# The second product of the last superblock by seven products of halves, transposed, and w_out's sums made from the second superblock on

## The chip, the cores and the metric

The kernel runs on one core of one Trainium2 chip. The metric is the device time of one execution in microseconds (us). PE is TensorE, ACT ScalarE, DVE VectorE, POOL GpSimd, and SP the engine whose queue issues all the transfers.

## What is computed

Chunk attention, then a feed-forward network with ELU, all in float32:

```
q, k, v: (8, 8, 576, 64)       chunks of 64 tokens, 8 heads
attn = softmax(q_c k_c^T / 8) over each chunk;  x = attn v_c   -> x: (4608, 512)
h = x @ w_in                   w_in: (512, 2048)
g = where(h > 0, h, exp(min(h, 0)) - 1)
out = g @ w_out                w_out: (2048, 512)
```

## The kernel before

**Tiling.** The 4608 tokens are 9 blocks of 512 (TB). A float32 product is made of three matmuls of rounded parts, high by high, high by low and low by high (`three`, L405): each operand X is kept as a cast hi and a difference lo = X - hi. The inner size 2048 is cut into 16 pieces f of 128 (NF), the model size 512 into 4 (NK).

**Stages.** The first three blocks are plain: for each f, `hidden` (L414) makes h with 12 matmuls of 512 columns, ACT and DVE make g (`elu`, L429), and `second_next` (L644) multiplies g by w_out for four token tiles, three matmuls each. The other six blocks form three superblocks of 1024 tokens (NS). There the first product is made by seven products of halves (Strassen's way, in Winograd's form) instead of eight. A pair g (class `Pair`, L596) stands for two pieces f; each of its seven products is 6 matmuls of 512 columns. The operands on w_in's side (sums of quarters) are made once by POOL in `combine` (L469), written to DRAM as `a_dram`, and loaded product by product (`load_a`, L531, line 533); those on x's side are made by `prepare` (L560). ACT copies products from PSUM (L629), DVE adds (L633), `elu_of` (L575) makes g, and `split_g` (L587) splits it, its cast on ACT (L588) and its low part (L590) on POOL or DVE.

**The second product** of a superblock is not reduced. Its first half of tokens is multiplied between the products of the pairs; its second half's g is kept in `g_kept` and multiplied after the eight pairs, under the list KEPT. `second` (L639) puts four products per f into a queue and `Q` in the lists takes the next one; eight items are still in the queue when a superblock ends, and the next one begins with them. The low half of w_out goes round through a ring of eight slices, loaded from `lo_dram` (`load_lo`, L546, line 549).

**Order.** The order of every engine except POOL's is written out by hand, in lists of items. One pair of a superblock follows

```
    PAIR = (
        "m p1 c1 4 E Q 4 z p2 d1 Q p6 c2 h 1 Q Q 1 p5 1 q k 1 Q l p7 c3 d2 Q Q 2 p4 c4 2 Q 3 p3 d3 "
        "3 3 3 s v x V"
    )
```

`p` is a product, `c` a copy, `d` an addition, `1` to `4` steps of g, `Q` a second product. The other letters are the attention of the next superblock's tokens, one tile of 128 per pair (class `Tokens`): m, E, z the softmax (L344 to L357), h the turn of the weights (L363 to L373), s the scores (L235), v the multiplication by v (L243), x its copy (L394), q and k the turns of q and k (L334), l and V the loads (L215, L199). In step h, DVE transposes blocks of 32 into `turned` (L366), ACT copies it into `unturned` (L369), and SP swaps blocks between partitions by four transfers of 32 KB, turned<-unturned (L373). PE's step v needs them. All transfers go out through SP in program order, so one that waits holds up those behind it. Loads of q and k are eight per tile (L215), sixteen where a tile crosses from one batch to the next (576 is not a multiple of 128).

The last superblock (from 667.76 us in the profile) has no attention left beside it. Its 24 left-over matmuls, 336 of the first product and 384 of the second follow the same lists. The finished tiles are copied from PSUM and stored as rows of 2 KB (`copy_out`, L446 to L449).

## Time and profile before

| | |
|---|---|
| median of 3 runs | 841.0 us (838.89 to 841.65) |
| span of the profiled execution, first to last instruction | 840.2 us |
| own time of the profiled execution beyond its span | not listed |
| PE busy | 826.3 us, 98% |
| DVE, ACT, POOL busy | 501.6, 480.4, 179.0 us |
| moved by DMA | 164.09 MB, 195 GB/s over the span |

Busy time is the time in which an engine has an instruction under way; matmuls overlap, so a busy PE says only that it was never empty. The chain of waits follows the work that ended last back to what released it. A window gives each engine's busy time between two moments.

### The profile page before, as it was taken

To read this page: it belongs to the slowest core of one execution; us is meant where nothing else is said; L and a number is where in the kernel's file an instruction comes from. 1 tells how busy PE (TensorE), PEld (TensorE's weight loads), DVE (VectorE), ACT (ScalarE), POOL (GpSimd) and SP (SyncE) were. 2 spreads that over 40 slices of the span, in tenths; PEclk is the share of its full clock that TensorE was granted. 3 is DMA by queue.
4 is the path that set the end of the run, shared out by engine and by line. 5 is a ranking of instruction groups with operands and counts; after the bars stand their busy time and mean duration, and the time that the engine had idled before them with its cause. 6 is when DMAs were issued, how large, how long until landed. Compare 5 with 4: busy or idle time off the path is not lost.

```text
span 840.2 us, 15685 instructions
## 1 busy us (share of the span) xinstructions
PE 826.3 (98%) x5949; PEld 677.0 (81%) x5949; DVE 501.6 (60%) x719; ACT 480.4 (57%) x825; POOL 179.0 (21%) x149
## 2 busy tenths in 40 slices
PE   7899999999999999999999999999999999999998
PEld 6788888887888888888888888778888888888886
DVE  4999997666775679565666746566555333233411
ACT  5999875444554547656666436655664355555521
POOL 0000014445312221111114521111126211111120
PEclk8999999999999999999999999999999999999999
DMA  9875754865787777698888656779844365545331
GB/s 240 263 228 187 247 181 152 271 205 183 232 234 218 207 193 218 191 258 239 241 240 242 191 149 200 199 233 257 238 146 138 111 198 160 164 144 163 101 101 50
DMA packets 178794, 164.09 MB, mean 195 GB/s; under 512 B 65568, under 2 KB 161312, under 8 KB 178720
## 3 DMA queue, kind: packets, MB, share of 16 engines
q1 hardware_dynamic: 178720, 163.10, 66.0%
q8 instruction: 47, 0.77, 0.4%
q14 instruction: 27, 0.22, 0.1%
HBM read 131.07 MB, written 28.31 MB: 190 GB/s over the span
## 4 chain that ended last, share of the span: by engine, by line
PE 92%; ACT 2%; DVE 2%; DMA 2%; SPq 1%; issue 1%; DVEq 0%; ACTq 0%
PE o L408 45%; PE h L408 40%; PE ps_a L235 2%; PE ps_a L243 2%; PE h L425 1%; DMA turned<-unturned 1%; SPq L199 1%; DMA k_sb<-in_k_dram 1%; PE ps_a L257 1%; PE ps_a L302 1%; SPq L373 0%; ACT st L135 0%; ACT a L280 0%; DVE e L435 0%; ACT e L433 0%
## 5 line engine op out<-in xcount | busy, mean ns | idle before, releaser
L408 PE MATMUL o<-wo_hi,ghi 128*128 128x512 f32 x416 | 163.8, 394 | 0.1
L408 PE MATMUL o<-wo_hi,glo 128*128 128x512 f32 x416 | 162.2, 390 | 0.0
L408 PE MATMUL o<-wo_lo,ghi 128*128 128x512 f32 x416 | 162.0, 390 | 0.0
L590 POOL TENSOR_TENSOR glo<-e,ghi 128x512 fp32r<-128x512 f32 x46 | 59.5, 1293 | 318.4 <-ACT ghi L588 318.4
L408 PE MATMUL h<-xhi,wi_hi 128*128 128x512 f32 x324 | 108.1, 394 | 0.0
L408 PE MATMUL h<-xlo,wi_hi 128*128 128x512 f32 x324 | 106.7, 389 | 0.0
L408 PE MATMUL o<-wo_hi,wo_lo 128*128 128x512 f32 x320 | 99.2, 389 | 0.0
L408 PEld LDWEIGHTS o<-wo_hi,ghi 128*128 128x128 f32 x416 | 78.1, 188 | 17.4 <-ACT ghi L440 0.5
L408 PEld LDWEIGHTS o<-wo_hi,glo 128*128 128x128 f32 x416 | 78.1, 188 | 16.7 <-DVE glo L443 0.4
L408 PEld LDWEIGHTS o<-wo_lo,ghi 128*128 128x128 f32 x416 | 78.1, 188 | 15.8
L629 ACT COPY kept<-h 128x512 f32<-128x512 f32 x72 | 42.2, 586 | 62.1 <-PE h L408 62.0
L408 PE MATMUL h<-wi_lo,wi_hi 128*128 128x512 f32 x288 | 75.0, 396 | 0.0
L408 PE MATMUL h<-wo_lo,wi_hi 128*128 128x512 f32 x288 | 72.9, 389 | 0.0
L408 PEld LDWEIGHTS h<-xhi,wi_hi 128*128 128x128 f32 x324 | 60.8, 188 | 12.9
L408 PEld LDWEIGHTS h<-xlo,wi_hi 128*128 128x128 f32 x324 | 60.8, 188 | 12.2
L408 PEld LDWEIGHTS o<-wo_hi,wo_lo 128*128 128x128 f32 x320 | 60.1, 188 | 12.5
L408 PE MATMUL h<-xhi,wi_lo 128*128 128x512 f32 x180 | 70.2, 390 | 0.0
L583 DVE SCALAR_TENSOR_TENSOR g_kept<-e,g_kept 128x512 f32<-128x512 f32 x48 | 33.2, 692 | 61.4 <-ACT e L580 61.4
L633 DVE TENSOR_TENSOR g_kept<-h,kept 128x512 f32<-128x512 f32 x48 | 33.1, 690 | 51.8 <-ACT kept L629 27.2
L408 PEld LDWEIGHTS h<-wo_lo,wi_hi 128*128 128x128 f32 x288 | 54.1, 188 | 11.2
L580 ACT ACTIVATE e<-e 128x512 f32<-128x512 f32 x96 | 60.7, 632 | 3.1
L408 PE MATMUL o<-wo_lo 128*128 128x512 f32 x160 | 62.2, 389 | 0.0
(114 smaller groups left out, 1330.3 us busy)
## 6 DMA issues: line engine op xcount, KB each, us to landing
wi_hi<-a_dram SPq DMA_DIRECT2D x168, 256.0 KB, 3.9
wo_lo<-lo_dram SPq DMA_DIRECT2D x52, 512.0 KB, 4.5
kept<-in_q_dram SPq DMA_DIRECT2D x100, 128.0 KB, 3.5
kept<-in_k_dram SPq DMA_DIRECT2D x100, 128.0 KB, 3.9
v_sb<-in_v_dram SPq DMA_DIRECT2D x32, 256.0 KB, 6.2
st<-in_moe_w_in_dram SPq DMA_DIRECT2D x16, 512.0 KB, 4.0
st<-in_moe_w_out_dram SPq DMA_DIRECT2D x16, 512.0 KB, 5.2
a_dram<-kept SPq DMA_DIRECT2D x16, 512.0 KB, 4.1
```

The costliest lines, as they stand in the source:

```text
L199: nc.sync.dma_start(out=dst[p0:p0 + n], in_=src[b, :, s0:s0 + n, :].rearrange("h s d -> s h d"))
L235: nc.tensor.matmul(scores[halves[c], j, hp, :], lhsT=qT[halves[j], hp, halves[c]], rhs=kT[halves[j], hp, halves[c]], start=True, stop=True,)
L243: nc.tensor.matmul(x_ps[halves[j], c, hp, :], lhsT=v_sb[halves[c], 2 * hp + j, :], rhs=aT[halves[c], :, j * NK + hp], start=True, stop=True,)
L257: nc.tensor.transpose(out=both[:, i, hp * P:(hp + 1) * P], in_=src[:, 2 * hp:2 * hp + 2, :], identity=ident,)
L302: nc.tensor.matmul(turned_ps[half, h, :], lhsT=a[half, h, :], rhs=ident[half, half], start=True, stop=True,)
L408: nc.tensor.matmul(ps, lhsT=a, rhs=b, start=start, stop=stop, skip_group_check=onto)
L425: nc.tensor.matmul(h, lhsT=w[:, kt, :], rhs=x[:, kt, :], start=i == 0, stop=i == len(terms) - 1)
L580: nc.scalar.activation(out=e, in_=e, func=AF.Exp, scale=-1.0)
L583: nc.vector.scalar_tensor_tensor(out=to, in0=e, scalar=-1.0, in1=c, op0=ALU.add, op1=ALU.max)
L590: engine.tensor_tensor(out=lo, in0=e, in1=hi.bitcast(F32), op=ALU.subtract)
L629: nc.scalar.copy(out=c21 if i == 4 else self.kept[i - 1], in_=x_ps)
L633: nc.vector.tensor_tensor(out=to, in0=y_ps, in1=self.kept[kept], op=ALU.add)
```

## The change

In the last superblock the second product too is made by seven products of halves: the token half and the two pieces f of a pair on g's side, two pieces f and two halves of the 512 columns on w_out's side. Each of the seven is 8 steps j (one per pair of pieces f) of 6 matmuls of 512 columns. w_out is the stationary operand now and g the moving one, so the result comes out transposed; DVE turns it back in blocks of 32, and to that end the columns of w_out are put in another order when it is first split (`in_order`), in all blocks. The stores of that superblock then have runs of 64 floats, in the last part of 32.

The operands on w_out's side go to a new DRAM tensor, `w_dram`. Three of the seven are raw quarters (`write_raw`, `write_raw_low`: 28 writes, item list RAW, beside KEPT of superblock 1). Four are sums (class `Sums`): for each j, POOL makes two additions of 512 columns and four subtractions of 256, ACT casts 1024 columns, DVE subtracts 1024, SP writes twice 512 KB. Those of j = 0 to 3 are made step by step in pairs 0 to 4 of superblock 1 (SUMS_AT; the writes fall behind `d2` of pairs 1 to 4), those of j = 4 to 7 at the start of the last superblock (`add_sums`).

The whole last superblock is no longer written out as a list. A class `Plan` collects jobs, each with reads, writes, an engine (or a choice of DVE and POOL) and a cost, and lays them out by list scheduling: PE in the given order, the others by the due time worked back from PE. POOL takes a job only when DVE is held by other work and the job isn't due soon, and the plan lets POOL and DVE not work at once on operations that share their way to the memory. All of the first product comes first (56 products of 6 matmuls), then the 56 steps of the second. All operands go through a ring of four entries of 512 KB (`load_entry`), loaded when the entry before has been used; the first four are loaded beside KEPT of superblock 1, in place of the loads of A there, and the last four loads of w_out's low half are no longer made. Four buffers are made differently without a change in size (`gp`, `io`), and POOL's order is by hand too from the third block on. Superblocks 0 and 1 otherwise keep their lists.

```diff
@@ -106,6 +106,10 @@
+    def in_order(w):
+
+        return w.rearrange("p (c b d) -> p b c d", b=4, d=Q)
+
...
+    HALF = DM // 2
+    w_dram = dram.tile([7, NG // 2, P, 2, 2, HALF], F32, name="w_dram")
+    W_OPS = (5, 6, 7, 4, 1, 2, 3)
+    W_PARTS = {1: (0, 0), 2: (1, 0), 3: (1, 1)}
...
 
+    class Sums:
+        def __init__(self, j: int, place, lows):
+            self.j, self.lows = j, lows
+            self.place = place.rearrange("p (l a) -> p l a", l=2)
+            self.w = self.place[:, 0].rearrange("p (i d) -> p i d", i=2)
+            self.s = self.place[:, 1].rearrange("p (i d) -> p i d", i=4)
+        def whole(self, i: int, engine=nc.gpsimd):
+            engine.tensor_tensor(
+                out=self.w[:, i], in0=w_out_slices(2 * self.j + i)[0].bitcast(F32),
+                in1=self.lows[i].bitcast(F32), op=ALU.add)
+        def sum(self, t: int, engine=nc.gpsimd):
+            b11, b12, b21, b22 = [self.w[:, i, c * HALF:(c + 1) * HALF]
+                                  for i in range(2) for c in range(2)]
+            t1, t2, t3, t4 = [self.s[:, i] for i in range(4)]
+            out, a, b = ((t1, b12, b11), (t2, b22, t1), (t3, b22, b12), (t4, b21, t2))[t - 1]
+            engine.tensor_tensor(out=out, in0=a, in1=b, op=ALU.subtract)
+        def high(self):
+            nc.scalar.copy(out=self.place[:, 0].bitcast(F32R), in_=self.place[:, 1])
+        def low(self, engine=nc.vector):
+            engine.tensor_tensor(
+                out=self.place[:, 1].bitcast(F32R), in0=self.place[:, 1], in1=self.place[:, 0],
+                op=ALU.subtract)
+        def write(self):
+            for lo in range(2):
+                nc.sync.dma_start(
+                    out=w_dram[:4, self.j // 2, :, self.j % 2, lo, :].rearrange("i p w -> p i w"),
+                    in_=self.place[:, lo].rearrange("p (i d) -> p i d", i=4))
...
+        def lows(j: int, half: int = 0):
+            return [weights[half][3][:, (2 * j + i) % (NF // 2), :] for i in range(2)]
+        for j, row in ((0, 8), (1, 12), (2, 8), (3, 12)):
+            yield j, lambda row=row: flat(g_kept[:, row:row + 4]), lows(j)
+    def write_raw(n: int, lo: int):
+        half, i = divmod(n, 3)
+        row, col = W_PARTS[i + 1]
+        for d in range(2):
+            nc.sync.dma_start(
+                out=w_dram[4 + i, 2 * half + d, :, :, lo, :],
+                in_=weights[half][2 + lo][:, 4 * d + row:4 * d + 4:2, col * HALF:(col + 1) * HALF].bitcast(F32))
+    def write_raw_low(j: int):
+        lows = weights[0][3][:, 2 * j % (NF // 2):][:, :2].bitcast(F32)
+        of = w_dram[:, j // 2, :, j % 2, 1]
+        nc.sync.dma_start(out=of[4], in_=lows[:, 0, :HALF])
+        nc.sync.dma_start(out=of[5:7].rearrange("i p d -> p i d"),
+                          in_=lows[:, 1].rearrange("p (i d) -> p i d", i=2))
     def flat(t):
         return t.rearrange("p a b -> p (a b)")
 
...
+    RAW = {0: "L0 L1", 1: "L2 L3", 2: "W0", 4: "W1", 6: "W2", 9: "L4 L5", 10: "W3", 11: "R0 L6", 12: "W4 R1",
+           13: "L7 W5", 14: "R2", 15: "R3"}
+    SUMS_AT = {0: ("p3",), 1: ("p1", "p2", "p6", "p5", "d2", "p4", "p3"),
+               4: ("p1", "p2", "c2", "d2"), 5: (), 6: (), 7: ()}
+    SUMS_AT[2] = SUMS_AT[3] = ("p1", "p2", "c2", "d2", "p4", "p3")
...
+    def load_entry(e: int):
+        slot, (phase, e) = ring_slot(e), divmod(e % ENTRIES, 7 * PAIRS)
+        if not phase:
+            d, o = divmod(e, 7)
+            for a in range(2):
+                nc.sync.dma_start(
+                    out=slot[:, a].bitcast(F32),
+                    in_=a_dram[2 * d + a, :, :, AOPS.index(PRODUCTS[FIRST[o]][0])])
+        else:
+            o, d = divmod(e, PAIRS)
+            nc.sync.dma_start(out=slot.bitcast(F32), in_=w_dram[W_OPS.index(SECOND[o]), d])
...
-    for s in range(NS):
-        n0 = (PLAIN + 2 * s) * TB
+    preparing, pair = True, None
+    for sb in range(2):
+        n0 = (PLAIN + 2 * sb) * TB
         run = n0, o_tiles(), a_half_place
...
-        preparing, kept = s + 1 < NS, iter(range(NF))
-        run = n0 + TB, o_tiles(), b_half_place
-        for line in KEPT:
-            for item in line.split():
+                if sb and item in SUMS_AT[g]:
+                    do("w")
+        halves_kept, o_last = iter(range(NF)), o_tiles()
+        run = n0 + TB, o_last, b_half_place
+        for f, line in enumerate(KEPT):
+            for item in line.split() + (RAW.get(f, "").split() if sb else []):
                 if item == "4":
                     next(pair.parts["4"], None)
                 elif item == "G":
-                    split_kept(next(kept))
+                    split_kept(next(halves_kept))
                 else:
                     do(item)
-    queue.sort(key=lambda item: item[2])
-    while queue:
-        second_next()
...
+    def product_second(i: int, j: int, e: int, s: int, to):
+        slot = ring_slot(e)[:, j % 2].rearrange("p l (i d) -> p l i d", i=2)
+        for c in range(2):
+            three(bank(to[c]), slot[:, 0, c], slot[:, 1, c], split_place(s, 0), split_place(s, 1),
+                  i in (1, 2, 4, 5) and j == 0, j == NG - 1, onto=i not in (1, 2, 4, 5))
...
+                if e == "POOL":
+                    at = max(port["DVE"], now)
+                    if at > now:
+                        return None, at
+                    aside = max(free["DVE"], now) + sum(
+                        jobs[i]["engines"]["DVE"][0] for i in ready["DVE"]
+                        if not jobs[i]["port"] and ready_at[i] <= now + POOL_NEAR)
+                    took = {i: jobs[i]["engines"]["POOL"][1] for i in mine}
+                    mine = [i for i in mine if aside >= now + POOL_SHARE * took[i] and (
+                        "DVE" not in jobs[i]["engines"] or jobs[i]["due"] >= now + POOL_MARGIN + 2 * took[i])
+                        or jobs[i]["due"] < now + 3000 and "DVE" not in jobs[i]["engines"]]
+                    if not mine:
+                        return None, later_on
+                if e == "DVE" and port["POOL"] > now:
...
+        def send():
+            for b in range(4):
+                at = b * P + c * 2 * Q
+                nc.sync.dma_start(
+                    out=out[n0:n0 + TB, at:at + 2 * Q].rearrange("(t p) d -> p t d", p=Q),
+                    in_=place()[b * Q:(b + 1) * Q].rearrange("p (t d) -> p t d", d=2 * Q))
+
...
+        def send(engine, which):
+            def run_():
+                for b in which:
+                    at = b * P + (2 + c) * Q
+                    engine.dma_start(
+                        out=out[n0:n0 + TB, at:at + Q].rearrange("(t p) d -> p t d", p=Q)[
+                            :, (cols.start or 0) // Q:cols.stop // Q],
+                        in_=place[b * Q:(b + 1) * Q])
...
+        block_of = {1: 0, 2: 1, 4: 3, 6: 3, 5: 0, 7: 2, 3: 1}
...
+            to = (x_, y_, z_)[banks_of[i]]
+            for j in range(NG):
+                k = NG * o + j
+                t, slot, b = t1 + k, k % NSPLIT, block_of[i]
...
+                ts = max(t - NSPLIT + .9, t1 + 1.2 if slot >= 4 else 0)
+                plan.add(ts, "ACT", ACT_OP, high, [("G", j, b)], [hi, lo])
+                plan.add(ts + .01, None, EITHER, low_, [("G", j, b), hi], [lo])
+                if i == 4:
+                    place2, place3 = [lambda j=j, b=b: g_place(j, b) for b in (3, 2)]
+                    place0, place1 = [lambda j=j, b=b: g_place(j, b) for b in (0, 1)]
+                    plan.add(ts + .1, None, EITHER, minus(place2, place2, place3),
+                             [("G", j, 2)], [("G", j, 3)])
+                    plan.add(ts + .2, None, EITHER, minus(place0, place0, place2, ALU.add),
+                             [("G", j, 3)], [("G", j, 0)])
+                    plan.add(ts + .3, None, EITHER, minus(place1, place1, place2),
+                             [("G", j, 3)], [("G", j, 1)])
...
+    for j in range(NG // 2, NG):
+        add_sums(T0 + 2 + 6 * (j - NG // 2), j)
+    for s in range(2, NS):
+        superblock(s)
+        if s + 1 < NS:
+            tokens(s)
+    plan.emit()
```

## Rows read from the trace of the kernel before

**Rows 1.** The page: first line, and busy us of PE

```profile
span 840.2 us, 15685 instructions
...
PE 826.3 (98%) x5949; PEld 677.0 (81%) x5949; DVE 501.6 (60%) x719; ACT 480.4 (57%) x825; POOL 179.0 (21%) x149
```

**Rows 2.** Waits of PE, 492 to 640 us: us, times, longest

```profile
PE ps_a L243 <- DMA turned<-unturned: 1.4, 3, 0.8
```

**Rows 3.** The chain of waits, whole span: start us, us, what

```profile
624.01 43.75 PE o L408 x192
...
787.44 49.03 PE o L408 x216
```

**Rows 4.** Windows: length, busy us, PEclk, DMA share, GB/s

```profile
667.76:787.44 119.68, 119.68 (x529) 99.13 (x529) 38.20 (x58) 66.52 (x112) 18.10 (x14) 1.00 0.51 153
```

**Rows 5.** Windows of pairs 2 to 5 of superblock 1, and a busy stretch

```profile
524.30:542.00 17.70, 16.86 (x135) 13.70 (x131) 10.38 (x17) 10.54 (x18) 2.95 (x3) 1.00 0.68 190
542.00:559.40 17.40, 16.81 (x131) 13.65 (x132) 10.11 (x16) 10.02 (x17) 2.35 (x3) 1.00 0.84 244
559.40:575.60 16.20, 16.20 (x131) 13.26 (x131) 9.83 (x16) 9.40 (x16) 2.45 (x2) 1.00 0.80 231
575.60:591.90 16.30, 16.30 (x135) 13.36 (x131) 10.13 (x17) 9.93 (x17) 2.59 (x2) 1.00 0.94 256
569.00:571.00 2.00, 2.00 (x11) 1.65 (x10) 2.00 (x4) 1.21 (x2) 1.11 (x1) 1.00 1.09 366
```

**Rows 6.** The chain of waits, 530 to 560 us

```profile
535.86 1.31 SPq L373
...
537.22 3.59 DMA turned<-unturned
...
553.72 4.82 DMA turned<-unturned
```

**Rows 7.** Timeline of SP, 515 to 590 us: start, us

```profile
522.95 5.24 SPq L215 DMA_DIRECT2D kept<-in_k_dram  x8
...
535.86 3.21 SPq L373 DMA_DIRECT2D turned<-unturned  x4
```

**Rows 8.** Operations by line, whole span: count, busy us, mean ns, idle before

```profile
L473 POOL TENSOR_TENSOR kept<-kept 128x256 f32<-128x256 f32 x32 | 29.2, 932 | 1.3
...
L473 POOL TENSOR_TENSOR kept<-wi_hi,wi_lo 128x512 f32<-128x512 f32 x16 | 21.3, 1350 | 157.4 <-DMA kept<-in_k_dram 117.2 <-DMA a_dram<-kept 40.1
L366 DVE STREAM_TRANSPOSE turned<-ps_a 128x512 f32<-128x512 f32 x28 | 20.1, 716 | 1.0
...
L502 DVE TENSOR_TENSOR kept<-kept 128x1024 fp32r<-128x1024 f32 x8 | 11.5, 1443 | 1.8 <-ACT kept L501 1.6
...
L172 ACT CAST wo_hi<-xf 128x512 fp32r<-128x512 f32 x16 | 10.0, 623 | 1.4 <-DVE xf L168 1.4
...
L590 DVE TENSOR_TENSOR wo_lo<-g_kept,wo_lo 128x512 fp32r<-128x512 f32 x11 | 7.6, 690 | 27.7 <-ACT wo_lo L588 27.7
```

**Rows 9.** Line L507, the writes of combine's sums: issue ns, and landing

```profile
L507 SPq DMA_DIRECT2D a_dram<-kept x16: 332/376/506, 153.0 to 257.9; - x16
...
DMA to landing us min/median/max: 2.8/4.1/6.0
```

**Rows 10.** Timeline of the end, 826 to 841 us

```profile
836.50 0.69 DVE L448 COPY g_kept<-o 128x512 f32<-128x512 f32 x1 [1.96 <-PE o L408]
```

**Rows 11.** Line L449, the last stores, from 780 us: issue ns, and landing

```profile
L449 SPq DMA_DIRECT2D out_dram<-g_kept x4: 332/334/337, 833.0 to 837.2; - x4
...
DMA to landing us min/median/max: 2.0/2.0/3.0
```

**Rows 12.** Line L199, whole span, loads of v: issue ns, and landing

```profile
L199 SPq DMA_DIRECT2D v_sb<-in_v_dram x40: 383/570/3506, 3.8 to 593.2; - x40
...
DMA to landing us min/median/max: 3.1/5.6/7.4
```

**Rows 13.** Line L443, the low part of g: ns min, median, max

```profile
L443 DVE TENSOR_TENSOR glo<-e,ghi x35: 642/692/1842, 35.6 to 322.7; 128x512 fp32r<-128x512 f32 x35
```

More of the change, by code (lines that the diff above doesn't have):

```diff
@@ new lines, in combine_w_out, with sums_by_hand @@
+    def combine_w_out():
+        for j, place, lows in sums_by_hand():
+            sums = Sums(j, place(), lows)
+            sums.whole(0)
+            yield
+            sums.whole(1)
+            yield
+            sums.sum(1)
+            sums.sum(3)
+            yield
+            sums.sum(2)
+            sums.sum(4)
+            yield
+            sums.high()
+            yield
+            sums.low()
+            sums.write()
+            yield
+    def sums_by_hand():
+        def lows(j: int, half: int = 0):
+            return [weights[half][3][:, (2 * j + i) % (NF // 2), :] for i in range(2)]
+        for j, row in ((0, 8), (1, 12), (2, 8), (3, 12)):
+            yield j, lambda row=row: flat(g_kept[:, row:row + 4]), lows(j)
@@ L593, in g_tiles @@
     def g_tiles():
-        return [gp.tile([P, TB], F32R, name=name) for name in ("ghi", "glo")]
+        return [place_of_g(F32R, name) for name in ("ghi", "glo")]
     class Pair:
@@ L843 @@
     later_w_out = w_out_tiles(wo1)
-    gp = ctx.enter_context(tc.tile_pool(name="gp", bufs=2, reuse_waits="tile"))
+    gp = ctx.enter_context(tc.tile_pool(name="gp", bufs=1, reuse_waits="tile"))
+    for i in range(6):
+        unit(i, F32, "unused")
     plain = ctx.enter_context(ExitStack())
@@ new lines, in add_attention, with now, score_, v_of @@
+    def add_attention(t: float, n: int, last: int):
+        tile_n = later.get(n)
+        this = {}
+        def now():
+            return later[n]
+        if n <= last:
+            def score_():
+                later[n].score()
+            plan.add(t, "PE", (590, 800), score_, ["qT", "kT"], ["psa"])
+        before = later.get(n - 1)
+        def v_of():
+            later[n - 1].times_v()
+        def x_of():
+            later[n - 1].keep()
+        half, part = divmod((n - 1) % (2 * NTT) ^ NTT, NTT)
+        cols = "a" if part < NTT - 1 else "b"
+        plan.add(t + .01, "PE", (590, 800), v_of, ["turned", ("v", (n - 1) % 2)], ["psa", "xps"])
+        plan.add(t + .7, "ACT", ACT_PSUM, x_of, ["psa", "xps"],
+                 [(name, part) for name in (("b11", "b21") if half == 0 else ("b12", "b22"))])
+        if n <= last:
+            add_softmax(t, n)
@@ new lines, in add_sums, with begin @@
+    def add_sums(t: float, j: int):
+        made = {}
+        def begin(engine):
+            made[0] = Sums(j, g_more_of(4 + j % 2), [weights[0][3][:, 2 * j + i - NF // 2, :] for i in range(2)])
+            made[0].whole(0, engine)
+        place = [("G", 4 + j % 2, b) for b in range(4)]
+        raw = [("s", i, l) for i in range(4) for l in range(2)] + [
+            ("G", i, b) for i in (6, 7) for b in range(4)]
+        half = {"DVE": (350, 423), "POOL": (700, 740)}
+        plan.add(t, None, EITHER, begin, raw, place[:1])
+        plan.add(t + .1, None, EITHER, lambda engine: made[0].whole(1, engine), raw, place[1:2])
+        for i, (k, reads) in enumerate(((1, ()), (3, ()), (2, (("t", j, 1),)), (4, (("t", j, 2),)))):
+            plan.add(t + .2 + .1 * i, None, half, lambda engine, k=k: made[0].sum(k, engine),
+                     [*place[:2], *reads], [("t", j, k)] + (place[2:] if k == 1 else []))
+        plan.add(t + .7, "ACT", (955, 1047), lambda: made[0].high(),
+                 [("t", j, k) for k in range(1, 5)] + place[2:], place[:2])
+        plan.add(t + .8, None, either(2 * TB), lambda engine: made[0].low(engine), place[:2], place[2:])
+        plan.add(t + .9, "SP", dma(2, 3200), lambda: made[0].write(), place, [("sums", j)])
```

632 lines of the change are left out of this document (573 added, 59 removed).

## The prediction, made before the change was run

> **What bounds the kernel now.** I read the page first: PE is busy 826.3 of 840.2 us and has 5949 matmuls [rows 1]; with so little idle time only two things can move the time, fewer matmuls or new waits of PE. The list of PE's waits comes second: in the pairs of superblock 1 it holds one entry, for the transfers turned<-unturned, 1.4 us in three places [rows 2]. The chain of waits comes third. It shows what a matmul of 512 columns costs in a row without a gap: 43.75 us for 192 and 49.03 us for 216 [rows 3], so 0.227 us. The last superblock begins at 667.76 (624.01 + 43.75) and its last matmul ends at 836.47 (787.44 + 49.03). By the code it holds 24 left-over matmuls, 336 of the first product and 384 of the second, 744 in all; 744 x 0.227 is 168.9 us against 168.7 measured. PE is busy 119.68 of 119.68 us in its first part [rows 4]. That stage is purely a count of matmuls, and ACT (66.5 us) and DVE (38.2 us) are half idle in it.
>
> The windows by pair of superblock 1 come fourth, since the change puts work there. Pairs 2 and 3 last 17.70 and 17.40 us, with PE busy 16.86 and 16.81; pairs 4 and 5 have no idle PE, though the DMA engines are busy 0.80 and 0.94 of the time [rows 5]. The chain around pairs 2 and 3 says why: PE stood before the multiplication with v until the four small swap transfers (L373) landed, 3.59 and 4.82 us after their issue [rows 6]. SP's timeline shows the cause: a token tile that crosses a batch costs 16 loads, whose second half alone takes 5.24 us, so that the swap goes out late and behind a full queue [rows 7].
>
> **The change, part by part.**
>
> *Fewer matmuls.* Seven products of halves in place of eight: 7 x 8 x 6 = 336 instead of 384. 48 x 0.227 = 10.9 us less, all of it on the path, because that stage has no gap.
>
> *The sums of w_out for j = 0 to 3, in pairs 0 to 4 of superblock 1.* POOL gets four times two additions of 512 and four subtractions of 256 columns: 4 x (2 x 1.35 + 4 x 0.93) = 25.7 us by the means of the same operations in combine [rows 8]. POOL worked 2.4 to 3.0 us per pair there [rows 5], so its idle time covers them. A glo can come up to four subtractions (3.7 us) late; the queue of second products ahead of it holds four to eight older items of 0.68 us each. Without that cover it is 1 to 2 us a pair. ACT's cast and DVE's subtraction (1.44 us, L502) [rows 8] fall into engines that idle over a third of a pair: nothing. What is not covered is the write: two transfers of 512 KB in each of pairs 1 to 4, 1 MB a pair. SP issues one such write in 0.38 us [rows 9], two in 0.75 us, and queued behind them stand the A operands, w_out's low half, v, and the next pair's swap, for which PE waits. The engines move at most 366 GB/s in a busy stretch [rows 5], so 1 MB takes 2.9 us, and whatever is issued behind it lands later by up to that. The price is 3.6 us where there is no slack, and pair 2 has none. Bounds: nothing (pair 5 ran at a share of 0.94 without a stall) and 3.6 us in each of pairs 2 to 5, 14.4 us. I take one full price, 3.6 us: pair 2 pays it, and its delay gives the transfers of the pairs behind it that time to catch up. Of the two ends it is nearer to the lower: pairs 2 and 3 stood still for under 1 us each at shares of 0.68 and 0.84, pair 5 not at all at 0.94, so a high share alone does not stop PE [rows 5].
>
> *The raw parts, written beside the last second product of superblock 1.* 12 + 16 writes and four ring entries of two loads, 36 issues of about 0.57 us, 21 us of SP in 43.75 us [rows 3]. They are 8 MB; four loads of w_out's low half and seven A operands are not made there any more, so 4.3 MB net, 97 GB/s more where 366 is possible. No attention runs there; PE needs from SP only low halves that are asked for several products ahead. Nothing; half of SP's time, some 10 us, would show if that lead were gone.
>
> *New column order of w_out (copies in groups of 32).* The cast into wo_hi takes 623 ns now; the transpose L366, which reads and writes such groups, takes 716 [rows 8]. Between 0 and 0.1 us an operation, 32 operations, nearly all under PE work: nothing taken, at most 1 us.
>
> *The last superblock as a planned order.* The second products no longer fill the first phase, so PE makes 360 matmuls in 81.7 us against ACT's 66.5 us of before (less 16 casts, plus 4 wider ones) [rows 4]; that fits. The sums j = 4 to 7 (on DVE 2 x 0.69, four halves of that and 1.44, about 4 us each) must be out of their places before the pairs that put G there, 28 steps of 1.36 us later, 38 us. In the second phase PE has 336 x 0.227 = 76.3 us. DVE has 56 low parts and 24 sums and differences of G at 0.69, 8 additions from PSUM at 0.69 and 6 transposes at 0.72 [rows 8]: 65 us, so DVE alone would do, with 11 us to spare. Operands come at 512 KB in 12 matmuls (2.72 us), 193 GB/s, three entries ahead (8 us); a transfer of that size lands in about 4 [rows 9]. I take 0.5 us for seams; bounds 0 and the third rival's 3.6.
>
> *The end.* Now 3.7 us lie between the last matmul and the span's end: copy 0.69, issue 0.33, landing 2.0, the rest 0.7 [rows 10, 11]. Then: a transpose of 0.72, four issues, landing, the same rest. With the issue and landing of v's loads in runs of 256 bytes (0.57 and at best 3.1, median 5.6 [rows 12]) it is 0.72 + 2.28 + 3.1 + 0.7 = 6.8; with today's stores (0.33 and 2.0) 4.8. So 1.0 to 3.1 us more, 5.6 with the median landing; I take 2.5, since four pieces of 64 KB overlap and the queue is empty by then. The Trainium skill, page "DMA: Bandwidth & Descriptors", section Specifications, speaks against these stores: under 512 bytes a transfer falls short of line rate, with read-modify-write. No store of this trace has runs as short as the new 128 to 256 bytes, so no row shows it; by the rule the end would lie at the upper bound, 5.6 us.
>
> **Sum.** -10.9 + 3.6 + 0.5 + 2.5 = -4.3 us. The profiled execution spans 840.2 us; its own time outside the span is not listed, and the median of the runs, 841.0, lies 0.8 above it, which I add as it is: 835.9 in the span, 836.7 as a time.
>
> **The rivals.**
>
> *The writes are hidden.* Pair 5 speaks for it: a share of 0.94 and no stall [rows 5]. Pair 2 with 1 MB more comes to about 0.85. Then -10.9 + 0.5 + 2.5: 833.1.
>
> *Slower: every swap of pairs 2 to 5 queues behind a write.* Place: SP's queue and the DMA rings behind it; price 3.6 us a pair. For it: landings of 3.59 and 4.82 us already stopped PE [rows 6], and pairs 3 and 4 come to shares near 1.0 with 1 MB more. Against it: pairs 4 and 5 have some slack now, and a late PE slows the demand. All four in full give 14.4 + 3.0 - 10.9 = +6.5 us, 847.5. It decides from 10.4 us on, that is from 2.6 us in each of the four pairs.
>
> *DVE and POOL stand in each other's way in the second phase.* In the trace DVE's glo takes 692 ns in the median and up to 1842 [rows 13], longer by 1.15 us, about one POOL operation. An operation that POOL takes over holds both for 1.29 instead of 0.69 us. DVE has 11 us to spare, used up when 18 of the 80 go to POOL; with all 24 sums and differences there, the last 6 cost PE 6 x 0.6 = 3.6 us on top of the forecast: 840.3. The Trainium skill, page "SBUF — State Buffer", section "Who interferes with whom", says that a DVE operation with two SBUF inputs and a GpSimd operation that reads SBUF exclude each other for a whole instruction. By that rule this rival would hold; the row of 1842 agrees, and the spare time speaks against its reaching PE.
>
> **How the numbers follow.** About 0.3%, 2.5 us, is what a measurement of this kernel can tell from no change, so faster means under 838.5 and slower over 843.5. Forecast (net gain 2.5 to 6 us) 0.42; writes hidden 0.20; two or three pairs paying, which lands between 838.5 and 843.5, 0.15; all pairs paying, slower, 0.13; DVE and POOL 0.10, mostly within 0.3%, a fifth of it slower. Faster 0.42 x 0.95 + 0.20, about 0.60; same about 0.22; slower about 0.18. The range runs from the hidden case with the short end (-10.9 + 1.0, 831.1) to where slower begins, 843.5; what is left out is the other side's upper part. The likeliest case's own range is 834.5 to 838.5.
>
> **What would show it.** Right: 48 matmuls fewer and an unbroken PE at 0.227 us behind superblock 1; pair 2 of superblock 1 longer by 3 to 4 us with PE waiting for turned<-unturned, later pairs by less; the end near 6 us with four small stores. The total would prove wrong if PE's waits for turned<-unturned stay near 1.4 us (hidden), or pass 10 us (slower); if PE waits for DVE or POOL behind 750 us (third rival); or if the ring's loads land after their products.

## The result, and the profile after

The time went up, from 839.7 us (838.84 to 841.65, 5 runs) to 844.8 us (842.1 to 845.0, 5 runs); ratio 1.005, interval 1.0032 to 1.0068. The forecast was 836.7 us in a range of 831.1 to 843.5, so it was wrong in its sign, and the time lies 1.3 us outside the range.

The page of the changed kernel, its first line and the busy times, answers to [rows 1]:

```profile
span 842.9 us, 15872 instructions
...
PE 816.8 (97%) x5901; PEld 666.0 (79%) x5901; DVE 581.8 (69%) x832; ACT 497.9 (59%) x853; POOL 185.8 (22%) x160
```

PE has 48 matmuls fewer and works 9.5 us less, as the change says; yet the span is 2.7 us longer. So new gaps of some 12 us must be found, and the waits of PE are the first view to ask. Between 492 and 640 us they were one entry of 1.4 us [rows 2]. Now they are:

```profile
PE h L434 <- DMA wi_hi<-a_dram: 5.6, 5, 2.1
PE ps_a L256 <- DMA turned<-unturned: 4.8, 5, 1.2
```

PE waits not only for the swaps (turned<-unturned, in the multiplication with v), but more still for the A operands of the first product (wi_hi<-a_dram). Where this happens is seen in windows over superblock 1 (length, then busy us of PE, PEld, DVE, ACT, POOL with their instructions, granted clock, share of the DMA engines, GB/s), to be laid beside [rows 5]:

```profile
508.00:524.30 16.30, 16.30 (x136) 13.36 (x131) 12.43 (x17) 10.82 (x18) 10.64 (x9) 1.00 0.65 182
524.30:542.00 17.70, 14.97 (x68) 11.82 (x65) 13.00 (x17) 10.88 (x18) 9.33 (x8) 1.00 0.86 213
542.00:560.00 18.00, 16.36 (x129) 12.93 (x128) 11.76 (x17) 9.67 (x16) 8.08 (x8) 1.00 0.93 254
560.00:576.00 16.00, 14.77 (x122) 11.72 (x120) 10.21 (x16) 9.20 (x16) 6.05 (x7) 1.00 0.88 235
576.00:592.00 16.00, 13.63 (x117) 10.95 (x117) 8.60 (x15) 8.24 (x14) 1.45 (x2) 1.00 0.90 255
592.00:608.00 16.00, 13.46 (x116) 10.55 (x115) 7.73 (x11) 8.45 (x15) 2.56 (x2) 1.00 0.91 253
608.00:624.00 16.00, 16.00 (x130) 13.13 (x129) 9.80 (x17) 9.93 (x17) 2.59 (x2) 1.00 0.78 241
```

PE is full up to 524 us and full again from 608 us on; in every window between, it stands still for 1.2 to 2.7 us, at a DMA share of 0.86 to 0.93. The granted clock is 1.00 in all of them, so none of the loss in this trace is a slower PE. Before, the same share or more went by without a gap (0.94 in pair 5 [rows 5]).

SP's timeline shows one of the four places where the sums are written (start us, us, instruction, count):

```profile
528.74 1.10 SPq L595 DMA_DIRECT2D w_dram<-g_kept  x2
529.92 1.01 SPq L650 DMA_DIRECT2D wi_hi<-a_dram  x1
...
534.28 4.28 SPq L650 DMA_DIRECT2D wi_hi<-a_dram  x3
538.65 3.54 SPq L399 DMA_DIRECT2D turned<-unturned  x4
```

The two writes go out at 528.74 us; the swap of the next tile is issued ten microseconds later, at 538.65 us, where before it went out at 535.86 [rows 7]. From issue to landing the swaps of this stretch take no longer than before (median 3.6 us, 3.7 before, between 524 and 610 us), so PE waits for them because they are issued late. The A operands do take longer to land: 7.4 us in the median between 524 and 608 us, 6.1 before, 5.2 in the kernel without the writes that is described below. The chain of waits (start us, us, what) runs through these writes:

```profile
529.38 8.57 DMA w_dram<-g_kept
...
540.30 4.04 DMA turned<-unturned
...
548.42 6.27 DMA w_dram<-g_kept
...
559.22 3.91 DMA turned<-unturned
...
569.17 8.04 DMA wi_hi<-a_dram
...
587.28 6.16 DMA w_dram<-g_kept
...
599.18 3.36 DMA turned<-unturned
...
635.48 47.16 PE o L434 x207
```

Before, such a chain came by the swaps alone, 3.59 and 4.82 us [rows 6]. The last line gives the total: the matmuls behind the eight pairs (KEPT) begin at 635.48 instead of 624.01 us [rows 3], 11.5 us later. The same list of superblock 0 begins at 464.58 us in both chains, so all of it is lost in the eight pairs.

The last superblock begins at 679.2 (635.48 + 43.75, the time of KEPT's 192 matmuls before [rows 3]). Its end in the chain, and in the view by line the last stores (issue ns, first and last start) and their landing, answer to [rows 10, 11]:

```profile
826.94 10.89 PE o L434 x48
837.84 0.02 issue
837.86 0.72 DVE g_kept L1626
```

```profile
L1633 SPq DMA_DIRECT2D out_dram<-g_kept x8: 316/492/545, 835.7 to 840.1; - x8
...
DMA to landing us min/median/max: 1.9/1.9/2.0
```

The last matmul ends at 837.8, so this stage has 158.6 us instead of 168.7; 5.1 us follow behind it instead of 3.7. The three differences make the sum: +11.5 - 10.1 + 1.3 = +2.7, from 840.2 to 842.9. The medians differ by more, 5.1 us. The profiled execution of after took 844.88 us, 2.0 more than its span. In the runs of before that were taken beside the experiments, the time lies 1.7 to 1.9 us beyond the span. By that, an estimate, the profiled execution of before took some 842.0 us, longer than all five runs above and 2.3 us over their median, which is the rest of the 5.1 us.

### The profile page after: what moved, and what is told of

It is laid out like the page before. It is cut to its first block, busy times and chain, and to the rows that moved or that the text cites. A ratio compares the mean times of both kernels' runs of the same rounds, so it can differ in the third digit from the quotient of the medians.

```text
span 842.9 us, 15872 instructions
## 1 busy us (share of the span) xinstructions
PE 816.8 (97%) x5901; PEld 666.0 (79%) x5901; DVE 581.8 (69%) x832; ACT 497.9 (59%) x853; POOL 185.8 (22%) x160
## 4 chain that ended last, share of the span: by engine, by line
PE 84%; DMA 7%; ACT 3%; SPq 3%; DVE 3%; issue 1%; DVEq 0%; ACTq 0%
PE o L434 44%; PE h L434 34%; DMA w_dram<-g_kept 2%; PE ps_a L248 2%; PE ps_a L256 2%; SPq L206 1%; DMA turned<-unturned 1%; PE h L451 1%; DMA w_dram<-g_more 1%; DMA wi_hi<-a_dram 1%; DMA st<-in_moe_w_in_dram 1%; SPq L227 1%; DVE g_more L574 1%; PE ps_a L315 1%; PE ps_a L270 0%
## 5 line engine op out<-in xcount | busy, mean ns | idle before, releaser
L434 PE MATMUL o<-wo_hi,ghi 128*128 128x512 f32 x352 | 139.0, 395 | 0.0
L434 PE MATMUL o<-wo_hi,glo 128*128 128x512 f32 x352 | 137.3, 390 | 0.0
L434 PE MATMUL o<-wo_lo,ghi 128*128 128x512 f32 x352 | 137.1, 390 | 0.0
L434 PEld LDWEIGHTS o<-wo_hi,glo 128*128 128x128 f32 x352 | 66.1, 188 | 14.4 <-DVE glo L479 0.4
L434 PE MATMUL o<-wo_hi,wo_lo 128*128 128x512 f32 x192 | 59.7, 390 | 0.0
L510 POOL TENSOR_TENSOR kept<-wi_hi,wi_lo 128x512 f32<-128x512 f32 x16 | 21.3, 1350 | 158.2 <-DMA kept<-in_k_dram 117.3
L471 DVE SCALAR_TENSOR_TENSOR e<-e,h 128x512 f32<-128x512 f32 x48 | 32.9, 685 | 27.1 <-ACT e L469 26.8
L434 PE MATMUL h<-wi_lo,wi_hi 128*128 128x512 f32 x192 | 50.6, 399 | 0.0
L434 PE MATMUL h<-wo_lo,wi_hi 128*128 128x512 f32 x192 | 48.5, 389 | 0.0
L361 DVE TENSOR_REDUCE mx<-ps_a 128x8 f32<-128x512 f32 x28 | 19.3, 689 | 39.7 <-ACT xf L420 39.0
L468 ACT ACTIVATE e<-h 128x512 f32<-128x512 f32 x48 | 28.7, 597 | 28.8 <-PE h L434 24.7
```

What stands on the lines that cost most here:

```text
L361: nc.vector.tensor_reduce(out=mx, in_=self.scores, axis=AX.X, op=ALU.max)
L434: nc.tensor.matmul(ps, lhsT=a, rhs=b, start=start, stop=stop, skip_group_check=onto)
L468: nc.scalar.activation(out=e, in_=h, func=AF.Relu, scale=-1.0)
L471: nc.vector.scalar_tensor_tensor(out=e, in0=e, scalar=-1.0, in1=h, op0=ALU.add, op1=ALU.max)
L510: nc.gpsimd.tensor_tensor(out=out, in0=a, in1=b, op=op)
```

## The experiments

**The theories.** Writes: the 4 MB that the first four sums write in pairs 1 to 4 hold up the loads and swaps behind them. Work: the additional work of POOL, DVE and ACT there delays g or the softmax, and the transfers are late because their data are. POOL's column of the windows (10.64, 9.33, 8.08 us where [rows 5] have 2.4 to 3.0) speaks for looking at it. All times below are medians; "before" is the kernel before, run on the same chip beside the kernels that are compared.

### The writes without the sums, the sums without the writes

The first kernel computes the sums of j = 0 to 3 and does not write them; the entries that would hold them are loaded from raw parts. The second writes them as after does, but leaves the computing of these sums out.

```diff
             sums.low()
-            sums.write()
...
-            nc.sync.dma_start(out=slot.bitcast(F32), in_=w_dram[W_OPS.index(SECOND[o]), d])
+            op = W_OPS.index(SECOND[o])
+            nc.sync.dma_start(out=slot.bitcast(F32), in_=w_dram[4 if op < 4 and d < 2 else op, d])
```

> The changed kernel with the sums of j = 0 to 3 still worked out in superblock 1, but their eight writes of 512 KB left out (the last superblock then multiplies by raw parts in their stead). Theory 'writes': what superblock 1 lost was lost to SP and the transfers queued behind these writes, so its pairs 2 to 6 go back to the length of before, PE's waits for turned<-unturned and for the A operands to under 2 us, and the time falls by 8 to 10 us, to 835 to 837. Rival 'work': it was lost to the sums' own work on POOL, DVE and ACT (DVE held up by POOL, casts ahead of the attention), so at least 6 of the 11 us stay and the time is 841 or more.

```diff
-            sums.whole(0)
             yield
-            sums.whole(1)
             yield
...
             yield
-            sums.low()
             sums.write()
```

> The opposite half: the writes are issued at the same places, but the additions, subtractions and casts for j = 0 to 3 are left out (whatever stands in those rows is written). 'Writes': nothing is regained beyond 2 us, 842 to 845, with pairs 2 to 6 as long as in the changed kernel. 'Work': pairs 2 to 6 go back, 834 to 837.

Without the writes 833.2 us, ratio 0.9906 (0.9888 to 0.9924); with the writes alone 845.3 us, ratio 1.0047 (1.0033 to 1.0061); before 841.0. The first falls below the 835 to 837 us that were expected, the second is as expected. The whole 12 us lie in the writes; for the work the runs show no cost. The windows of the first show pairs 2 and 3 full, with all of POOL's work in them:

```profile
524.30:542.00 17.70, 17.57 (x165) 13.89 (x164) 14.12 (x18) 11.61 (x20) 9.90 (x9) 1.00 0.65 184
542.00:560.00 18.00, 17.95 (x165) 14.70 (x166) 14.43 (x20) 10.66 (x18) 9.35 (x8) 1.00 0.92 257
```

The second window stands at a share of 0.92 without a stall; with the writes it had 0.93 and 1.6 us of idle PE. The mean share does not tell the two apart. In the second kernel PE's waits from 492 to 640 us are nearly those of after, although POOL is busy 16.8 us in the seven windows instead of 40.7:

```profile
PE h L434 <- DMA wi_hi<-a_dram: 5.0, 3, 2.5
PE ps_a L256 <- DMA turned<-unturned: 3.6, 4, 1.1
PE h L434 <- ACT e L704: 1.2, 1, 1.2
```

### The swaps on ACT's queue

If the swaps only queue behind the writes in SP's program order, another queue frees them. The edit was made to the changed kernel and to the kernel before.

```diff
-                    nc.sync.dma_start(out=turned[to, 1 - e], in_=unturned[of, e])
+                    nc.scalar.dma_start(out=turned[to, 1 - e], in_=unturned[of, e])
```

> The changed kernel with the four swap transfers turned<-unturned issued from ACT's queue, right behind the copy that they read, in place of SP's. If the swap's place in SP's queue, behind the writes and loads, is what PE pays for, its wait for turned<-unturned falls from 4.8 us to under 1 and the time by 4 to 8 us, to 837 to 841. If the amount of data is the limit (all 16 engines busy about 0.9 of the time in pairs 2 to 6), PE waits for the A operands instead and the gain is under 2 us. 'Work': no change, or slower by ACT's four issues per tile, some 2 us.

> The control: the same move of the swaps to ACT's queue in the kernel before. It has only 1.4 to 2 us of waiting for swaps, so 837.5 to 840: at most 2 us less; more than that less, and the queue held up more than its trace shows; slower, and the issues on ACT cost something themselves.

Both miss by far: 932.7 us, ratio 1.110 (1.107 to 1.113), and in the kernel before 925.4 us, ratio 1.100 (1.099 to 1.102). The view by line of the latter shows the issues (ns min, median, max), and ACT's timeline one tile:

```profile
L373 ACTq DMA_DIRECT2D turned<-unturned x112: 514/602/1256, 143.8 to 698.2; - x112
```

```profile
530.57 0.62 ACT L369 COPY unturned<-turned 128x512 f32<-128x512 f32 x1 [5.12 <-DVE turned L366]
531.22 2.44 ACTq L373 DMA_DIRECT2D turned<-unturned  x4
533.76 0.62 ACT L588 CAST wo_lo<-g_kept 128x512 fp32r<-128x512 f32 x1 [2.57 <-DMA turned<-unturned]
```

The swaps landed well (1.9 us in the median, 2.1 before), but an issue takes 602 ns of ACT itself, four of them 2.44 us a tile, and what ACT does next for PE is late by that. This is only a part of the 84.4 us. PE is idle for some 57 us more, and its largest waits in that kernel (us, times, longest) are for ACT, for the turn of k and for A operands:

```profile
PE h L408 <- ACT kept L629: 22.5, 13, 2.3
PE ps_a L235 <- DVE k_turned L334: 15.0, 9, 5.5
PE h L408 <- DMA wi_hi<-a_dram: 9.4, 2, 5.3
PE o L408 <- ACT ghi L440: 7.1, 4, 2.1
```

In the other 27 us PE is busy: it takes 853.2 us for the same 5949 matmuls instead of 826.3, at a mean granted clock of 0.968 instead of 0.995. After a wait of 4.15 us, for example, the granted clock is 0.50, the lower of its two levels, and six matmuls take 2.90 us (a window of 3 us):

```profile
601.40:604.40 3.00, 2.94 (x7) 2.39 (x8) 1.15 (x2) 0.01 (x1) 1.27 (x1) 0.50 0.70 204
```

So ACT's queue is no way out here. Yet the two kernels, laid side by side, say something on the theories. In neither does PE wait for a swap any more, and still KEPT of superblock 1 begins 13.9 us later in the changed kernel (the first fence) than in the other (the second). Each fence has the line of the chain for KEPT and PE's waits for A operands between 530 and 720 us:

```profile
721.80 49.20 PE o L434 x216
...
PE h L434 <- DMA wi_hi<-a_dram: 21.3, 7, 5.8
```

```profile
707.90 43.75 PE o L408 x192
...
PE h L408 <- DMA wi_hi<-a_dram: 4.2, 1, 4.2
```

With the swaps out of SP's queue the loss remains, now at the A operands, which stay on SP behind the writes. Whether it is the order on that queue or the time that the writes take from the DMA engines, this pair can't tell.

### What it is in the writes: issues, bytes, or where they go

Four kernels change the writes, the eight of j = 0 to 3 above all. Where a sum is not wholly written, the ring loads raw parts in its place, as in the first experiment.

Only 8 KB of each write, so that issue, place and wait stay:

```diff
...
+                    nc.sync.dma_start(
+                        out=w_dram[0, self.j // 2, :, self.j % 2, lo, :16],
+                        in_=self.place[:, lo, :16])
...
```

> All eight writes of superblock 1 are issued at their places and wait for the same subtraction, but each moves only 8 KB (16 columns) of the sums. 'Bytes': 833 to 835, as without writes. 'Issue': SP's 1.1 us a pair and its wait for DVE's subtraction are what PE pays for, 840 to 845.

Only the high halves, four writes of 512 KB:

```diff
-            for lo in range(2):
+            for lo in range(1 if self.j < NG // 2 else 2):
...
```

> The changed kernel with only the high half of each sum of j = 0 to 3 written (one write of 512 KB in place of two; the last superblock multiplies by raw parts in their stead). Without any of these writes the time was 833.2, with all of them 844.8: 11.6 us for 4.2 MB. Theory 'bytes' (the transfers queue up behind what the writes move, about 2.9 us per MB): half the bytes cost half, 838 to 840. Rival 'issue' (SP's time for two more issues a pair, 1.1 us): about half too, so the next run tells these two apart. Rival 'tipping' (the queue holds until the engines' share passes one): under a third stays, 834 to 836.

All bytes, into a tensor in which the four sums of a partition stand behind one another, 128 rows of 4 KB a write instead of 512 of 1 KB (nothing is left out; all sums, those of the last superblock too, go there and are loaded from there):

```diff
+    s_dram = dram.tile([NG // 2, P, 2, 2, 4, HALF], F32, name="s_dram")
...
-                    out=w_dram[:4, self.j // 2, :, self.j % 2, lo, :].rearrange("i p w -> p i w"),
-                    in_=self.place[:, lo].rearrange("p (i d) -> p i d", i=4))
+                    out=s_dram[self.j // 2, :, self.j % 2, lo].rearrange("p i w -> p (i w)"),
+                    in_=self.place[:, lo])
...
```

> The same bytes in another form: the sums are written to a DRAM tensor of their own whose rows are 4 KB long, 128 pieces a write in place of 512 pieces of 1 KB; the last superblock's loads of them then come in pieces of 1 KB. Theory 'bytes alone': no change, 843 to 846. Rival 'form': the writes land in 5.4 to 8.6 us where combine's, with rows of 4 KB, land in a median of 4.1, so pieces of 1 KB make them slow; then landing falls towards 4 us and the time by 3 to 6 us, to 839 to 842.

A quarter of each row, 512 rows of 256 bytes a write:

```diff
...
+                        out=w_dram[:4, self.j // 2, :, self.j % 2, lo, :64].rearrange("i p w -> p i w"),
+                        in_=self.place[:, lo].rearrange("p (i d) -> p i d", i=4)[:, :, :64])
...
```

> In the changed kernel each write of the sums of j = 0 to 3 keeps its 512 pieces but moves a quarter of the bytes, pieces of 256 bytes in place of 1 KB (the last superblock multiplies by raw parts in their stead). Rows of 4 KB regained 7.3 of the 11.6 us at the same bytes. Theory 'pieces' (a write takes the engines by its number of pieces): most of the loss stays, 840 or more. Theory 'bytes, with a cost per piece beside': about 835 to 837. If the bytes alone count, 833 to 835, and then the form of 4 KB must have helped in another way.

| writes of j = 0 to 3 | us | ratio to before (interval) | median landing of one, us |
|---|---|---|---|
| as changed, 1 KB rows | 844.8 | 1.0050 (1.0032 to 1.0068) | 8.1 |
| 8 KB each | 833.0 | 0.9908 (0.9883 to 0.9932) | 4.3 |
| high halves only, 1 KB rows | 836.2 | 0.9962 (0.9944 to 0.9981) | 7.2 |
| all, 4 KB rows | 837.5 | 0.9963 (0.9945 to 0.9981) | 5.2 |
| a quarter, 256-byte rows | 834.8 | 0.9933 (0.9911 to 0.9955) | 3.7 |

Eight issues, with their place in SP's order and their wait for DVE, show no cost (833.0 against 833.2 without any). The bytes do it: half of them cost 3 to 5 us of the 12 (by medians or by ratios). In proportion it would be a ratio of 0.998, just inside the interval, so whether a threshold lies there is not settled. As many rows with a quarter of the bytes cost 2 us, so the number of rows alone isn't the price. The form matters as much as half of the bytes: all of them in 4 KB rows cost some 4.5 us instead of 12, and the 837.5 us lie below the 839 to 842 that were expected for that case. The DMA lists of after and of the kernel with 4 KB rows (KB each, median us to landing):

```profile
w_dram<-g_kept SPq DMA_DIRECT2D x8, 512.0 KB, 8.1
```

```profile
s_dram<-g_kept SPq DMA_DIRECT2D x8, 512.0 KB, 5.2
```

and the latter's waits of PE from 492 to 640 us, where the A operands are almost gone and the swaps stay:

```profile
PE ps_a L256 <- DMA turned<-unturned: 3.7, 3, 1.4
PE h L434 <- DMA wi_hi<-a_dram: 1.0, 3, 0.4
```

That form differs in two things: rows of 4 KB instead of 1 KB, and one place for the four sums of a partition, where the changed kernel sends each of the four into its own part of `w_dram`, 2 MB from the next. Two more kernels part them. One keeps the changed kernel and puts 4 KB between the parts, in case a distance of a power of two does the harm; the other takes the tensor of the 4 KB rows and leaves a gap of 256 bytes behind each sum, so that the rows are of 1 KB again but the four of a partition lie together, within 5 KB. Neither leaves anything out.

```diff
-    w_dram = dram.tile([7, NG // 2, P, 2, 2, HALF], F32, name="w_dram")
+    w_rows = dram.tile([7, NG // 2 * P + 1, 2, 2, HALF], F32, name="w_dram")
+    w_dram = w_rows[:, :NG // 2 * P].rearrange("i (d p) a l w -> i d p a l w", p=P)
```

> The changed kernel with one edit: the seven parts of w_dram lie 2 MB and 4 KB apart in place of 2 MB, so that the four parts of a write no longer lie a power of two apart. Nothing is left out, rows stay 1 KB. If the distance of a power of two is what makes the writes dear (12 us), the time falls towards that of the 4 KB rows, 836 to 839 us, and the landing of w_dram<-g_kept from 8.1 to 5 or 6 us. If it is the length of the rows, or that they lie far apart at all, it stays at 843 to 846 us with a landing near 8 us and waits of PE near 10 us in the pairs of superblock 1.

```diff
-    s_dram = dram.tile([NG // 2, P, 2, 2, 4, HALF], F32, name="s_dram")
+    s_dram = dram.tile([NG // 2, P, 2, 2, 4, HALF + 64], F32, name="s_dram")
...
```

> The kernel with 4 KB rows (837.5 us) with one edit: in the tensor of the sums every row of 1 KB is followed by 256 unused bytes, so that a write has 512 rows of 1 KB again, which lie near one another. Nothing is left out. If the length of a row is what counts, the time rises to that of the changed kernel, 843 to 846 us, and the landing of s_dram<-g_kept from 5.2 to 7 or 8 us. If it is the distance of the four parts, it stays at 835 to 839 us with a landing of 5 to 6 us.

With padded parts 847.1 us, ratio 1.0075 (1.0051 to 1.01), landing 8.1 as before the edit: the distance of exactly 2 MB between the parts is not it. (Its median lies 2.3 us above that of the changed kernel, but the intervals of the two ratios overlap; and in its trace the granted clock falls to a mean of 0.93 in the window from 524.3 to 542 us, where the changed kernel had 1.00.) With short rows that lie together 837.4 us, ratio 0.9962 (0.9945 to 0.9978): the same as with 4 KB rows, and the landing is even shorter:

```profile
s_dram<-g_kept SPq DMA_DIRECT2D x8, 512.0 KB, 4.6
```

So it is not the length of a row. What costs the difference, 7 to 8 of the 12 us, is where the rows lie: the four of a partition in four parts 2 MB apart, with 4 KB from one partition to the next in each, instead of the four within 5 KB and 20 KB from one partition to the next (16 KB with rows of 4 KB). The two distances change together, so the runs don't say which of them counts. The sums of the last superblock have changed their place too, but the gain is made before them: KEPT begins at 627.96 us (4 KB rows) and 630.51 us (short rows) instead of 635.48, and what follows lasts 207.1 and 206.6 us, 207.4 in the changed kernel.

### The writes where nobody waits, and both together

If the place is the fault, the writes need only move. j = 0 is now made and written earlier (pair 0); j = 1 is made in pair 1 and written in pair 5 behind p5; j = 2 and 3 are made by DVE beside KEPT, where there is no attention. Nothing is left out.

```diff
...
-        for j, row in ((0, 8), (1, 12), (2, 8), (3, 12)):
+        for j, row in ((0, 8), (1, 12), (2, 0), (3, 4)):
...
-    SUMS_AT = {0: ("p3",), 1: ("p1", "p2", "p6", "p5", "d2", "p4", "p3"),
-               4: ("p1", "p2", "c2", "d2"), 5: (), 6: (), 7: ()}
-    SUMS_AT[2] = SUMS_AT[3] = ("p1", "p2", "c2", "d2", "p4", "p3")
+    SUMS_AT = {0: ("p1", "p2", "p6", "p5", "p7", "p4"), 1: ("p1", "p2", "p6", "p5", "p7"), 2: (), 3: (), 4: (),
+               5: ("p5",), 6: (), 7: ()}
```

> The whole change, with the sums at other times: j = 0 in pair 0 (its write behind p4, engines' share 0.54 there), j = 1 in pair 1 but written in pair 5 behind p5, j = 2 and 3 on DVE beside KEPT of superblock 1, where no attention runs, in rows of g_kept whose g has been used. If what was lost is the bytes in pairs 1 to 4, three of the four MB are out of the way: PE's waits in pairs 2 to 6 under 3 us, 834 to 837, faster than both kernels. If the work or its place matters otherwise (the low parts of g late beside KEPT), 838 or more.

832.9 us, ratio 0.9913 (0.9886 to 0.994); the time is that of the kernel without writes (833.2), though the writes landed in 7.1 us, hardly faster. Of PE's waits from 492 to 640 us, 1.6 us for swaps and 0.6 us for ACT are left. One of them, 0.7 us between 592 and 608 us, comes behind the two scattered writes that pair 5 still has. The last kernel has this order and the 4 KB rows:

> Both mendings together: the sums at other times (832.9 alone) and written in rows of 4 KB (837.5 alone). Moved, one write a pair at most stands before a swap; with 4 KB rows it costs less still, so 831.5 to 833.5. If the form matters by its effect on the queue in general, beside KEPT and in the last superblock too, under 832; if the 16 loads in pieces of 1 KB come too late in the last superblock, above 833.5.

831.7 us (830.1 to 831.8), before 840.6; ratio 0.989 (0.9872 to 0.9908). It has the lowest median of all kernels here, though its interval overlaps with that of the order alone. Of PE's waits from 492 us to the end one is left, and the windows that lost 2.7 and 1.6 us are full:

```profile
PE h L434 <- ACT kept L763: 0.2, 1, 0.2
```

```profile
524.30:542.00 17.70, 17.70 (x196) 14.54 (x196) 11.25 (x18) 10.31 (x18) 2.59 (x2) 1.00 0.70 199
542.00:560.00 18.00, 18.00 (x138) 14.74 (x139) 10.52 (x18) 11.15 (x20) 3.32 (x3) 1.00 0.88 246
```

## Why the prediction was wrong

**The step that failed** is "The sums of w_out for j = 0 to 3, in pairs 0 to 4 of superblock 1", at its sentence "I take one full price, 3.6 us". Measured are 11.5 us in the trace and 12 us by leaving the writes out. The place, the resource and the upper bound (14.4) were right; the rival on the other side, "every swap of pairs 2 to 5 queues behind a write", is nearest to what happened, and its point of decision (10.4 us in sum) was passed by 1 us (its time, 847.5, is 2.7 us above the measured one). Three things in the working were off:

- *How many pairs pay.* I let pair 2 pay and its delay set the others free. It did not: in the trace all of the windows from 524 to 608 us pay, 11.5 us over four written pairs or 2.9 each, so the count was wrong. The 2.9 us are a mean and not the price of one pair: where only pair 5 had scattered writes, at another place in the pair, the wait behind them was 0.7 us. The argument for the lower end was that pair 5 ran at 0.94 without a gap [rows 5]. A mean share over a pair was the wrong measure: at 0.92 PE was full without the writes, at 0.93 it stood with them.
- *Who pays.* I counted the swaps, with the A operands among what queues behind a write. In the trace the A operands were the larger wait, 5.6 against 4.8 us.
- *Which row gave the price.* It rested on rows of another form: the writes of [rows 9], landing in 4.1 us, are combine's sums, which lie together in DRAM, and 366 GB/s is a stretch of other traffic [rows 5]. The new writes are scattered and landed in 8.1 us; put together, in the same place of the order, they landed in 4.6 to 5.2 and cost some 4.5 us, not far from the 3.6 I took.

**What held.** *Fewer matmuls*: the last superblock is 10.1 us shorter; with -10.9 for the matmuls, 0.8 are left for *the last superblock as a planned order*, where I had 0.5. The window from its start (columns as above) shows PE full to 0.4 us:

```profile
679.00:837.80 158.80, 158.40 (x698) 130.32 (x696) 118.06 (x183) 93.40 (x159) 9.92 (x8) 1.00 0.70 221
```

*The raw parts* and *the new column order*: nothing, as forecast; KEPT goes on without a gap into the next stage, 207 matmuls in 47.16 us, 0.228 each. *The end*: +1.3 instead of +2.5, within the bounds of 1.0 and 5.6. The stores landed in 1.9 us like the rows of 2 KB (2.0 [rows 11]); I should have taken the low value, from a store, and not have leant on loads of v, which land in a busier stretch. The Trainium skill, page "DMA: Bandwidth & Descriptors", section Specifications, has transfers under 512 bytes short of line rate, with read-modify-write; by that rule I had 5.6 us. The stores of 64 KB in 128-byte runs did not land late, so the rule did not decide the end; they are a quarter of the size of those before, so the trace doesn't show whether they moved at line rate.

*From span to time*: I added 0.8 us, the distance from the span of one execution, by the estimate above a long one, to the median of others. The runs of after lie 1.9 to 2.0 above their own spans (844.79 and 842.8, 844.88 and 842.9), so about 1.1 us more was missing. That is small beside the 8 us of the failed step.

**The rivals.** *The writes are hidden* gave 833.1 us: the kernel without writes needs 833.2 and the one that moves them 832.9, so that its number was right, only not for this order. In part that is luck: the span without the writes fell by 8.4 us (840.2 to 831.8) and not by 7.9, and its time lies 1.8 us above it and not 0.8. *DVE and POOL stand in each other's way in the second phase* did not happen: POOL has hardly any work in it, and DVE's low parts and sums stay near their 0.69 us (the slowest group of them averages 0.75); two groups from 755 us on (count, busy us, mean ns, idle before):

```profile
L1436 DVE TENSOR_TENSOR g_more<-g_more 128x512 f32<-128x512 f32 x13 | 8.7, 681 | 0.0
L1718 DVE TENSOR_TENSOR split<-g_kept,split 128x512 fp32r<-128x512 f32 x12 | 8.3, 689 | 4.4 <-ACT split L1715 4.4
```

In superblock 1, beside POOL's sums, the lengthening is there (one step of g, line 716, takes 725 ns in the median and 1780 at most between 508 and 600 us, and at most 694 where the sums are not made), and the first two experiments show that it costs nothing: taking the writes away brings all of the time back, taking the work away none.

## What to carry to other kernels

Before a transfer is called hidden, find the next transfers behind it for which PE waits, and ask what becomes of their issue and their landing: the mean share of the DMA engines over a stage does not tell whether a stage has room. Take the price of a write from a row that goes to DRAM in the same pattern, not from one of the same size, and lay a tensor out so that the rows of one write lie together, even if its loads then come in shorter pieces. And when a saving is real but its preparation sits where the queue is tight, move the preparation first: the same writes cost 12 us in one place and, in another, nothing that the times show.

## What the runs showed of the hardware that was not expected

The same 512 KB, written at the same place of SP's order, land in 8.1 us when their 512 rows of 1 KB are scattered over four parts of a tensor, in 4.6 us when the four rows of a partition lie together, and in 5.2 us as 128 rows of 4 KB; the kernel's time differs by 7 to 8 us between the first and the other two. The landing depends on the other traffic too: with the swaps on ACT's queue and a slower kernel the same scattered writes took 5.3 us. The Trainium skill, page "DMA: Bandwidth & Descriptors", section "Latency and other measured facts", knows slow copies at a row pitch that is a large power of two, cured by a pad of a few KB. Here 4 KB of pad between the parts brought no gain (8.1 us, 847.1 against 844.8 us), so this is not shown to be the same effect. Why rows that lie like this are dear, and which of the two distances (2 MB between the parts, 4 KB within one) counts, the runs leave open; so too why PE loses 12 us to writes that take only a few us longer each.

The loads that match the gathered form come in 1 KB pieces and land in 3.7 to 4.5 us in the median of each kernel, where the changed kernel's loads of w_dram took 3.2, without a stop of PE in the last superblock of the fastest kernel.

The same 112 swaps issued from ACT's queue made the kernel 84 us longer, though the transfers themselves landed no later than from SP (1.9 against 2.1 us): some 57 us of idle PE, and some 27 us in which PE was busy for longer with the same matmuls, at a mean granted clock of 0.968 instead of 0.995.
